# One exponential of 2048 columns for 20 score visits, and a second order of all queues, in a two-layer attention and MLP kernel

## The chip, the cores and the metric

The kernel runs on one core of a Trainium2 chip. The engines are named as in the profile: PE multiplies matrices, ACT evaluates functions, DVE and POOL work on vectors, and SP issues the DMAs. Each engine works through a queue of its own, and semaphores hold an instruction until what it needs is there. The metric is the device time of one execution in microseconds, the median over several runs. Lower is better.

## The reference

Two layers run over a sequence of 2048 tokens with 512 features, with the same weights in both. A layer is sliding-window attention with 32 heads of 16 features, where a token sees itself and the 255 before it, and then an MLP with 1792 hidden features. Each has a layernorm ahead and adds its result to x.

```python
def _A_ref(x, wqkv, wo):
    H = 32; Dh = D // H; W = 256
    qkv = (x @ wqkv).reshape(B, S, 3, H, Dh).transpose(2, 0, 3, 1, 4)
    scores = jnp.einsum("bhqd,bhkd->bhqk", q, k) * (Dh ** -0.5)
    mask = (idx[:, None] - idx[None, :] >= 0) & (idx[:, None] - idx[None, :] < W)
    p = softmax(jnp.where(mask, scores, -1e9))
    return jnp.einsum("bhqk,bhkd->bhqd", p, v)... @ wo
def _B_ref(x, w1, b1, w2, b2):
    return gelu(x @ w1 + b1) @ w2 + b2
for layer in range(2):
    x = x + _A_ref(_layernorm(x), A_wqkv, A_wo)
    x = x + _B_ref(_layernorm(x), B_w1, B_b1, B_w2, B_b2)
```

## The kernel before

The 2048 tokens are 16 tiles of 128, and two layers make 32 tiles, or 16 blocks of 256 tokens (blocks 0 to 7 are layer one). x stays on the core in X for the whole run, as do all weights after their load. The work of a block b is:

- layernorm of its tiles on DVE and POOL (statistics at L628, normalized tile xn at L650), then a transpose to xnTA, by PE for the first four tiles and by a DMA of SP for the others (L655);
- projections to Q and K (512 columns of PSUM, half of the features each) and to V. QT is copied out by DVE or ACT (L617, L619). KT is copied by DVE with a product with `parmask` (L710), which writes it twice, once with the even and once with the odd heads kept. Va is V; Vs is V shifted by half a tile, made by two DMAs a tile (L725);
- scoring "visits" (`visit`, L758): a visit fills 512 columns for each of four row groups of PE, so four banks of PSUM: a pair gA and a pair gB. L777 are its matmuls. Two exponentials follow on ACT, of 128 x 1024 elements each, one a pair (L784), into the ring E, and then masks on DVE or POOL (L805). A block has ten visits, the first block of a layer five;
- two value products a block (`pv`, L829), each over half of the heads, then transposes, a division by the sums (L838 to L852), the output projection, and the sum into X (L878);
- the MLP in ten jobs of two or four tiles: first product with W1, bias on DVE and gelu on ACT (L901, L904), or both in one activation (L909), then the product with W2 and the sum (L921), in the second layer with a store of the tile by SP.

PSUM has eight banks, shared by all of this. ACT must load a table whenever it changes between exponential and gelu.

Nothing is ordered at run time. The kernel first records all its operations as nodes in the order of the source, and tables at the top of the file then decide: `_ORDER` gives the sequence in which nodes enter their engines' queues, `_ALT` the nodes that go to a second engine (a mask to POOL, a copy to ACT), `_BANKS` the PSUM bank of each allocation, `_TURNS` extra dependencies between two nodes. `_PAD` lists matmul groups that get two more waits ahead of them on PE. Both are on a semaphore value that has long been reached, so they only move the instructions behind them within the pages in which PE's program is fetched. `_Plan.run` applies the tables, and `_Sched.op` derives the waits from what each node reads and writes. At most eight DMAs of SP are open at a time, since each waits for the one eight places ahead.

The code around the scores and the evacuation of K is where the change acts:

Of the kernel before, what the change touches and what calls it, by code (L numbers as in the profile page):

```python
# [7 lines left out]
ALU = mybir.AluOpType  # L8
# [11 lines left out]
class _Sched:  # L20
# [347 lines left out]
]  # L368

_PAD = [  # L370
    127, 761, 1289, 1123, 1124, 1116, 1197, 1673, 1403, 1404, 1405, 1406, 1231, 1250, 1251, 1433, 1556,
]

_BANKS = [
# [75 lines left out]
def bass_interleave_layers__sliding_block__dense_activation_gelu__prompt_kernel(  # L450
# [13 lines left out]
    P = 128  # L464
# [34 lines left out]
    with ExitStack() as kctx:  # L499
# [112 lines left out]
        def piece(cuts, fc):  # L612
            return [lo <= fc < hi for lo, hi in cuts].index(True)
# [390 lines left out]
```

## Time and profile before

| | us |
|---|---|
| median of 3 runs | 433.87 (433.02 to 435.62) |
| the profiled execution's own time | 433.44 |
| its span, first to last instruction | 431.7 |
| PE busy | 410.6 |
| ACT busy | 379.6 |
| DVE busy | 336.0 |
| POOL busy | 217.3 |

Busy time is summed over the span. Matmuls are pipelined, so PE counts as busy also where it runs below its peak. The granted clock of PE was 1.0 in the profiled run. The costliest groups on the other engines are the 300 exponentials (282.4 us of ACT) and the masks (128.3 us on POOL, 49.2 us on DVE). The span in 40 slices, in tenths:

```profile
PE   8978999998999989999999999999999999999997
ACT  2898999999999999999998999999977998998523
DMA  7994412201201114010121211011221004102120
```

PE and ACT are both close to full for most of the span. ACT has room at the start and in the last slices, and the DMA engines are in use mostly in the first tenth, while x and the weights are loaded.

### The profile page before, as it was taken

To read this page: it belongs to the slowest core of one execution; us is meant where nothing else is said; L and a number is where in the kernel's file an instruction comes from. 1 tells how busy PE (TensorE), PEld (TensorE's weight loads), DVE (VectorE), ACT (ScalarE), POOL (GpSimd) and SP (SyncE) were. 2 spreads that over 40 slices of the span, in tenths; PEclk is the share of its full clock that TensorE was granted. 3 is DMA by queue.
4 is the path that set the end of the run, shared out by engine and by line. 5 is a ranking of instruction groups with operands and counts; after the bars stand their busy time and mean duration, and the time that the engine had idled before them with its cause. 6 is when DMAs were issued, how large, how long until landed. Compare 5 with 4: busy or idle time off the path is not lost.

```text
span 431.7 us, 16809 instructions
## 1 busy us (share of the span) xinstructions
PE 410.6 (95%) x7500; PEld 228.0 (53%) x7571; DVE 336.0 (78%) x637; ACT 379.6 (88%) x447; POOL 217.3 (50%) x242
## 2 busy tenths in 40 slices
PE   8978999998999989999999999999999999999997
PEld 4655847644544445463554555465545554444763
DVE  5998897889978778857899687779767675857941
ACT  2898999999999999999998999999977998998523
POOL 5576555466444585435764462613537347332420
PEclk9999999999999999999999999999999999999999
DMA  7994412201201114010121211011221004102120
GB/s 229 297 162 107 125 38 44 51 3 41 58 21 33 26 28 74 20 29 2 40 47 26 34 39 41 17 25 29 56 45 27 2 17 78 50 2 72 43 74 24
DMA packets 49059, 23.50 MB, mean 54 GB/s; under 512 B 34268, under 2 KB 48988, under 8 KB 48988
## 3 DMA queue, kind: packets, MB, share of 16 engines
q1 hardware_dynamic: 48988, 22.43, 22.9%
q8 instruction: 59, 0.97, 0.9%
q14 instruction: 12, 0.10, 0.1%
HBM read 8.00 MB, written 2.10 MB: 23 GB/s over the span
## 4 chain that ended last, share of the span: by engine, by line
PE 68%; ACT 19%; DVE 7%; issue 2%; DMA 1%; POOL 1%; SPq 1%; DVEq 0%
PE ps L676 53%; ACT E L784 15%; PE ps L777 7%; PE ps L829 6%; PE ps L569 2%; ACT gT L909 1%; DMA Vs<-Va 1%; DVE OD L838 1%; ACT gT L904 1%; DVE E L805 1%; DVE QT L617 1%; POOL Nb L846 1%; ACT L909 1%; DVE stat L628 1%; DVE KT L710 1%
## 5 line engine op out<-in xcount | busy, mean ns | idle before, releaser
L784 ACT ACTIVATE E<-ps 128x1024 bf16<-128x1024 f32 x300 | 282.4, 1044 | 18.6 <-PE ps L777 17.8
L805 POOL TENSOR_TENSOR E<-E,mask 128x512 bf16<-128x512 bf16 (+2 forms) x116 | 128.3, 1120 | 105.2 <-DVE E L805 50.4
L676 PE MATMUL ps<-W_sb,gT 128*128 128x512 bf16 x413 | 105.6, 380 | 4.6 <-issue 3.7
L676 PE MATMUL ps<-xnTB,W_sb 128*128 128x512 bf16 (+1 forms) x547 | 101.7, 336 | 1.7 <-issue 0.8
L676 PEld LDWEIGHTS ps<-xnTB,W_sb 128*128 128x128 bf16 x560 | 52.4, 98 | 42.9 <-issue 1.6
L676 PE MATMUL ps<-xnTA,Wqkv_sb 128*128 128x256 bf16 x512 | 67.5, 273 | 1.3 <-DVE xnTA L617 0.5
L777 PE MATMUL ps<-QT,KT 32*128 32x128 bf16 (+3 forms) x1920 | 60.1, 231 | 3.1 <-ACT E L784 1.4
L676 PEld LDWEIGHTS ps<-W_sb,gT 128*128 128x128 bf16 x448 | 38.3, 98 | 43.7 <-issue 4.0
L805 DVE TENSOR_TENSOR E<-E,mask 128x512 bf16<-128x512 bf16 (+2 forms) x120 | 49.2, 434 | 15.0 <-POOL E L805 6.6
L676 PEld LDWEIGHTS ps<-xnTA,Wqkv_sb 128*128 128x128 bf16 x512 | 47.4, 98 | 17.9 <-issue 2.5
L777 PEld LDWEIGHTS ps<-QT,KT 32*128 32x128 bf16 x1920 | 28.2, 92 | 50.5 <-ACT E L784 31.9
L838 DVE STREAM_TRANSPOSE OD<-ps 128x1024 f32<-128x1024 f32 x32 | 39.7, 1242 | 12.2 <-PE ps L829 12.0
L909 ACT ACTIVATE gT<-ps,b1T 128x512 bf16<-128x512 f32 (+1 forms) x80 | 43.0, 605 | 5.6 <-PE ps L676 5.2
L917 POOL TENSOR_TENSOR Xb<-X,b2all 128x512 f32<-128x512 bf16 x32 | 36.8, 1153 | 18.8 <-DVE X L921 12.0
L628 DVE BATCH_NORM_STATS2 stat<-X 128x6 f32<-128x512 bf16 x64 | 43.2, 682 | 2.8 <-DMA X<-in_A_x_dram 2.1
L901 DVE TENSOR_SCALAR gT<-ps,b1T 128x512 bf16<-128x512 f32 (+1 forms) x60 | 36.5, 634 | 7.0 <-PE ps L676 6.6
L829 PE MATMUL ps<-E,Va 64*17 64x192 bf16 (+3 forms) x1920 | 39.5, 230 | 2.2 <-ACT E L784 1.0
L710 DVE TENSOR_TENSOR KT<-ps,parmask 128x1024 bf16<-128x1024 f32 x32 | 38.8, 1212 | 3.4 <-PE ps L676 2.9
L829 PE MATMUL ps<-E,Vs 64*17 64x128 bf16 (+3 forms) x1920 | 38.8, 230 | 0.0
L846 POOL TENSOR_TENSOR Nb<-OD,Rc 128x512 bf16<-128x512 f32 x21 | 22.2, 1056 | 32.5 <-DVE Rc L842 16.0
L650 DVE TENSOR_SCALAR xn<-X,statmv,rstd 128x512 bf16<-128x512 bf16 x64 | 24.4, 402 | 13.4 <-POOL rstd L640 8.3
L921 DVE TENSOR_TENSOR X<-Xb,ps 128x512 bf16<-128x512 f32 x32 | 21.5, 677 | 17.0 <-PE ps L676 16.7
(49 smaller groups left out, 358.2 us busy)
## 6 DMA issues: line engine op xcount, KB each, us to landing
Vs<-Va SPq DMA_DIRECT2D x64, 68.0 KB, 2.1
W_sb<-in_B_w_dram SPq DMA_DIRECT2D x4, 512.0 KB, 4.9
out_dram<-X SPq DMA_DIRECT2D x16, 128.0 KB, 1.8
X<-in_A_x_dram SPq DMA_DIRECT2D x3, 512.0 KB, 6.2
Wqkv_sb<-in_A_wqkv_dram SPq DMA_DIRECT2D x4, 256.0 KB, 6.1
W_sb<-in_B_w_dram SPq DMA_DIRECT2D x2, 384.0 KB, 7.9
W_sb<-in_B_w_dram SPq DMA_DIRECT2D x1, 768.0 KB
Wqkv_sb<-in_A_wqkv_dram SPq DMA_DIRECT2D x1, 512.0 KB, 7.0
```

The costliest lines, as they stand in the source:

```text
L628: add("dve", lambda e, B, t=t, k6=k6: e.bn_stats(stat6[:, k6, :], X[:, t, :]), reads=["X%d" % t], writes=["st%d" % k6], key="bs%d" % (k + j))
L676: r = e.matmul(ps[:, B[g][0], cols], lhsT, rhs, start=st, stop=sp)
L710: add("dve", lambda e, B, g=g, i=i: e.tensor_tensor(out=KT[:, kb, 2 * i : 2 * i + 2].rearrange("p c m a q -> p a (c m) q"), in0=ps[:, B[g] ...
L777: x = e.matmul(ps[:, bk[r], o : o + n], KT[rows, kb, c, m].rearrange("p a q -> p (a q)"), QT[rows, c, q : q + n], start=True, stop=True)
L784: add("act", lambda e, B, g_=g_, gi=gi: e.activation(E[:, 2 * gi : 2 * gi + 2, e0 : e0 + 512], ps[:, B[g_][0] : B[g_][0] + 2, :], AF.Exp, ...
L805: fn = lambda e, B: e.tensor_tensor(out=Ew, in0=Ew, in1=Mw, op=ALU.mult)
L829: x = e.matmul(ps[32 * r : 32 * r + VW, B[g][par], c % 2 * 2 * P + lo : c % 2 * 2 * P + hi], V[rows, (2 * b + m // 2) % VR, c * HC + 2 * r ...
L838: add("dve", lambda e, B: e.transpose(OD[:, s].rearrange("p a c q -> p (a c q)"), ps[:, B[g][0] : B[g][0] + 2, :]), reads=["ps:" + g], wri ...
L846: return e.tensor_tensor(out=Nb[:, s, :].rearrange("p (k a d) -> p a k d", a=2, d=Dh), in0=sums[:, :, :, 0:Dh], in1=rc[:, :, :, None].to_b ...
L901: add("dve", lambda e, B, g=g, fc=fc: e.tensor_scalar(out=gT[:, fc, c0 : c0 + M], in0=ps[:, B[g][0], 0:M], scalar1=b1T[:, fc : fc + 1], sc ...
L909: add("act", lambda e, B, g=g, fc=fc: e.activation(gT[:, fc, c0 : c0 + M], ps[:, B[g][0], 0:M], AF.Gelu_apprx_tanh, bias=b1T[:, fc : fc + ...
L917: add("pool", lambda e, B, t=t, xs=xs: e.tensor_tensor(out=Xb[:, xs, :], in0=X[:, t, :], in1=b2all[:], op=ALU.add), reads=["X%d" % t, "b2a ...
```

## The change

There are five parts.

1. Twenty visits, listed in `_WHOLE`, have one exponential of 2048 columns over all four banks in place of two of 1024. Their banks are used in rising order. The pairs may lie apart, so the access steps from one pair to the other.
2. The copy of K may go to ACT, as two activations with `parmask` as scale, one for each parity. One of the 32 does: the first half of block 0.
3. The second MLP product of tile 31, its sum and its store are split into two halves of 256 columns, with a group of 14 matmuls each.
4. All tables are new: order, second engines, turns, pads and banks. Pads go from 17 to 9. Four more copies of V go to ACT (12 instead of 8), six more masks and one more division to POOL.
5. In the new order of SP the larger weight loads stand behind the first shifts of V and transposes.

The number of table loads on ACT stays 18. The visits of `_WHOLE` are counted over the whole program; the first eight (11, 12, 13, 24, 34, 42, 47, 64) belong to blocks 1 to 6.

```diff
+_WHOLE = [
+    11, 12, 13, 24, 34, 42, 47, 64, 71, 72, 88, 89, 90, 91, 97, 119, 126, 127, 135, 144,
+]
 _PAD = [
-    127, 761, 1289, 1123, 1124, 1116, 1197, 1673, 1403, 1404, 1405, 1406, 1231, 1250, 1251, 1433, 1556,
+    228, 230, 232, 188, 189, 472, 646, 668, 734,
 ]
...
+                def kcopy(e, B, g=g, i=i):
+                    for a in range(2):
+                        x = e.activation(
+                            KT[:, kb, 2 * i : 2 * i + 2, :, a, :].rearrange("p c m q -> p (c m) q"),
+                            ps[:, B[g][0], :].rearrange("p (k q) -> p k q", q=HK), AF.Copy, scale=parmask[:, a : a + 1])
+                    return x
...
-                    reads=["ps:" + g, "parmask"], writes=names, free=[g], key="ke%d_%d" % (b, i))
+                    reads=["ps:" + g, "parmask"], writes=names, free=[g], key="ke%d_%d" % (b, i), alt=(("act", kcopy),))
...
+                whole = first[b] + g in _WHOLE
...
-                    bk = tuple(B[gA]) + tuple(B[gB])
+                    bk = tuple(sorted(tuple(B[gA]) + tuple(B[gB]))) if whole else tuple(B[gA]) + tuple(B[gB])
...
-                for gi, g_ in enumerate((gA, gB)):
+                if whole:
+                    def ex(e, B):
+                        lo, hi = sorted((B[gA][0], B[gB][0]))
+                        d = max(1, (hi - lo) // 2)
+                        return e.activation(
+                            E[:, :, e0 : e0 + 512].rearrange("p (z r) q -> p z r q", z=2),
+                            ps[:].rearrange("p (z r) q -> p z r q", r=2)[:, lo // 2 : hi // 2 + 1 : d],
+                            AF.Exp, scale=SCALE)
+
+                    add("act", ex, reads=["ps:" + gA, "ps:" + gB], writes=grains(e0, 512, "ab"), free=[gA, gB],
+                        key="ex%d_%d_0" % (b, g))
+                for gi, g_ in enumerate(() if whole else (gA, gB)):
...
+                parts = 2 if tau == NT - 1 else 1
+                for z in range(parts):
+                    u, lo, hi = tau + z, D // parts * z, D // parts * (z + 1)
...
```

**The start, on DVE.** The rows are line, operation, what is written and read, and its size; lines of the new file are some three higher up to L660. The queue of DVE from its first instruction, before:

```order
L567 MEMSET gT 128x256
L628 BN_STATS stat<-X 128x6
L630 BN_AGGR statmv<-stat 128x2
L551 TENSOR_SCALAR pidx<-pidx 128x2
L628 BN_STATS stat<-X 128x6
L630 BN_AGGR statmv<-stat 128x2
L628 BN_STATS stat<-X 128x6 x2
L650 TENSOR_SCALAR xn<-X,statmv,rstd 128x512 x2
```

and now:

```order
L570 MEMSET gT 128x256
L631 BN_STATS stat<-X 128x6
L633 BN_AGGR statmv<-stat 128x2
L554 TENSOR_SCALAR pidx<-pidx 128x2
L637 TENSOR_SCALAR rstd<-statmv 128x1
L631 BN_STATS stat<-X 128x6
L633 BN_AGGR statmv<-stat 128x2
L653 TENSOR_SCALAR xn<-X,statmv,rstd 128x512
L637 TENSOR_SCALAR rstd<-statmv 128x1
L631 BN_STATS stat<-X 128x6
```

The first normalized tile stands ahead of the third tile's statistics, and the sum with epsilon (L637) has come over from POOL.

**The start, on PE.** The queue of PE from its first matmul: warm-up matmuls on zeros (from gT), transposes (from ident), projections (from Wqkv_sb), scores (from QT, KT). Before:

```order
L569 MATMUL ps<-gT 128x512 x18
L662 MATMUL ps<-ident,xn 128x128 x8
L676 MATMUL ps<-xnTA,Wqkv_sb 128x256 x8
L662 MATMUL ps<-ident,xn 128x128 x8
L676 MATMUL ps<-xnTA,Wqkv_sb 128x256 x18
L777 MATMUL ps<-QT,KT 128x256 x8
```

and now:

```order
L572 MATMUL ps<-gT 128x512 x12
L665 MATMUL ps<-ident,xn 128x128 x4
L572 MATMUL ps<-gT 128x512
L665 MATMUL ps<-ident,xn 128x128 x4
L572 MATMUL ps<-gT 128x512 x3
L679 MATMUL ps<-xnTA,Wqkv_sb 128x256 x16
L665 MATMUL ps<-ident,xn 128x128 x8
L679 MATMUL ps<-xnTA,Wqkv_sb 128x256 x4
L788 MATMUL ps<-QT,KT 128x256 x8
```

Some warm-up matmuls stand behind the first transposes (two more far behind), sixteen projections instead of eight stand ahead of the second transposes, and the first scoring visit comes after 20 projections instead of 26.

**The start, on ACT and SP.** The queue of ACT from its first instruction, before:

```order
L619 ACT_TABLE_LOAD
L619 ACTIVATE xnTA<-ps 128x4x128 x2
L619 ACTIVATE QT<-ps 128x2x256
L784 ACTIVATE E<-ps 128x2x512
L619 ACTIVATE QT<-ps 128x2x256
L784 ACTIVATE E<-ps 128x2x512 x12
```

and now:

```order
L622 ACT_TABLE_LOAD
L622 ACTIVATE xnTA<-ps 128x4x128
L715 ACTIVATE KT<-ps,parmask 128x8x64 x2
L622 ACTIVATE xnTA<-ps 128x4x128
L806 ACTIVATE E<-ps 128x2x512 x2
L622 ACTIVATE QT<-ps 128x2x256 x2
L806 ACTIVATE E<-ps 128x2x512 x18
```

The two halves of the first K copy stand between the two copies of xnTA, and the first two exponentials stand ahead of two query copies, one of which came over from DVE. SP's queue behind the loads of Wqkv, before:

```order
L577 DMA X<-in_A_x_dram 128x4x512
L598 DMA W_sb<-in_B_w_dram 128x4x512
L596 DMA Wo_sb<-in_A_wo_dram 128x4x512
L607 DMA W_sb<-in_B_w_dram 128x3x512
L598 DMA W_sb<-in_B_w_dram 128x4x768
L725 DMA Vs<-Va 64x544
L655 DMA_TRANSPOSE xnTA<-xn 128x4x128 x2
L725 DMA Vs<-Va 64x544 x3
```

and now:

```order
L735 DMA Vs<-Va 64x544 x2
L580 DMA X<-in_A_x_dram 128x4x512
L658 DMA_TRANSPOSE xnTA<-xn 128x4x128 x2
L735 DMA Vs<-Va 64x544 x2
L599 DMA Wo_sb<-in_A_wo_dram 128x4x512
L735 DMA Vs<-Va 64x544 x2
L658 DMA_TRANSPOSE xnTA<-xn 128x4x128 x2
L601 DMA W_sb<-in_B_w_dram 128x4x512 x2
```

Five loads of x and weights stood ahead of the first shift of V; now they stand behind it.

**Blocks 9 and 10, on ACT.** ACT's queue mostly for the second layer, from the table load behind the gelus of the fourth MLP job to the gelus of the fifth; E is written by exponentials, Va is a copy of V, QT one of Q. Before:

```order
L784 ACT_TABLE_LOAD
L784 ACTIVATE E<-ps 128x2x512 x2
L619 ACTIVATE QT<-ps 128x2x256
L784 ACTIVATE E<-ps 128x2x512 x16
L619 ACTIVATE Va<-ps 128x32x16
L784 ACTIVATE E<-ps 128x2x512 x6
L619 ACTIVATE Va<-ps 128x32x16
L784 ACTIVATE E<-ps 128x2x512 x14
L904 ACT_TABLE_LOAD
```

and now:

```order
L806 ACT_TABLE_LOAD
L806 ACTIVATE E<-ps 128x2x512 x18
L622 ACTIVATE Va<-ps 128x32x16
L806 ACTIVATE E<-ps 128x2x512 x4
L622 ACTIVATE Va<-ps 128x32x16
L806 ACTIVATE E<-ps 128x2x512 x2
L622 ACTIVATE Va<-ps 128x32x16
L806 ACTIVATE E<-ps 128x2x512 x6
L798 ACTIVATE E<-ps 128x4x512 x4
L931 ACT_TABLE_LOAD
```

Both hold the exponentials of the same 19 visits. The copy of Q has gone to another engine, a third copy of V has come, and the last four visits have merged exponentials (128x4x512), one behind the other.

More of the change, by code (lines that the diff above doesn't have):

```diff
@@ L918, in mlp @@
                     reads=["X%d" % t, "b2all"], writes=["Xb%d" % xs], key="xb%d" % tau)
[L919 to L926 removed]
+                parts = 2 if tau == NT - 1 else 1
+                for z in range(parts):
+                    u, lo, hi = tau + z, D // parts * z, D // parts * (z + 1)
+                    g = "y%d" % u
+                    pe_group(g, [(gT[:, fc, c0 + i * P : c0 + (i + 1) * P], W2_sb[:, fc, lo:hi], slice(lo, hi),
+                                  fc == 0, fc == FC - 1) for fc in range(FC)], 1,
+                             [gn(fc) + ["W2_%d" % piece(W2_CUTS, fc)] for fc in range(FC)], key=g)
+                    add("dve", lambda e, B, g=g, t=t, xs=xs, lo=lo, hi=hi: e.tensor_tensor(
+                        out=X[:, t, lo:hi], in0=Xb[:, xs, lo:hi], in1=ps[:, B[g][0], lo:hi], op=ALU.add),
+                        reads=["Xb%d" % xs, "ps:" + g], writes=["X%d" % (t + z)], free=[g], key="ya%d" % u)
+                    if tau >= NT - T:
+                        dma(lambda e, B, t=t, lo=lo, hi=hi: e.dma_start(out[0, t * P : (t + 1) * P, lo:hi], X[:, t, lo:hi]),
+                            ["OUT%d" % (t + z)], reads=["X%d" % (t + z)], key="out%d" % (t + z))
         nextjob = 0
```

8 lines of the change are left out of this document (removed), and 408 rows, old and new, of tables (_ALT, _BANKS, _ORDER, _TURNS).

## The prediction

> **What bounds the kernel now.** I read the page's busy shares first, then its chain of work, then the busy times in four stretches that I cut at the first exponential (12.79 us), at the last exponential that the second value product of block 6 needs (165.50) and at the last value product (401.70). In the stretches each engine has its busy time and, in brackets, its instructions.
>
> ```profile
> PE 410.6 (95%) x7500; PEld 228.0 (53%) x7571; DVE 336.0 (78%) x637; ACT 379.6 (88%) x447; POOL 217.3 (50%) x242
> PE 68%; ACT 19%; DVE 7%; issue 2%; DMA 1%; POOL 1%; SPq 1%; DVEq 0%
> 0.00:12.79 12.79, 11.03 (x69) 6.01 (x70) 8.24 (x23) 3.08 (x5) 6.08 (x20) 1.00 0.84 245
> 12.79:165.50 152.71, 143.05 (x2987) 84.51 (x3009) 131.21 (x248) 148.96 (x177) 90.28 (x96) 1.00 0.31 70
> 165.50:401.70 236.20, 229.64 (x4171) 120.17 (x4196) 182.03 (x339) 217.60 (x245) 113.61 (x120) 1.00 0.17 36
> 401.70:431.70 30.00, 26.84 (x294) 17.28 (x296) 14.49 (x30) 9.96 (x23) 7.35 (x7) 1.00 0.14 41
> ```
>
> Two engines take turns. From 12.79 to 165.50 ACT works 148.96 of 152.71 us, 97.5%, and PE 94%: here ACT sets the pace. From 165.50 on PE is at 97% and ACT at 92%: here PE sets it. The rest of PE's order behind the boundary is fixed work, so time saved on ACT before 165.50 moves the end, and time lost by ACT afterwards costs nothing until ACT's results come too late. The waits of ACT in the two middle stretches (microseconds in total, times, longest) say how much there is to take away:
>
> ```profile
> ACT E L784 <- PE ps L777: 4.4, 8, 0.8
> ACT E L784 <- PE ps L777: 13.4, 27, 1.1
> ```
>
> The first row is the early stretch, the second the late one. So in the paced stretch at most 4.4 us of waiting could go; whatever else is gained there must come from less work on ACT or an earlier start. That is why I expect a change of under one per cent.
>
> **The change part by part, against the profiled execution's own 433.44 us** (span 431.70; the rest, 1.74 us, lies around it and is kept). The median of the three runs is 0.43 us above it.
>
> *The start.* The timeline of DVE, ACT, PE and SP at the start:
>
> ```profile
> 2.17 0.47 SPq L582 DMA_DIRECT2D Wqkv_sb<-in_A_wqkv_dram  x1
> 5.08 1.29 DVE L628 BATCH_NORM_STATS2 stat<-X 128x6 f32<-128x512 bf16 x2 [0.31 <-DMA X<-in_A_x_dram]
> 6.28 0.72 DVE L650 TENSOR_SCALAR xn<-X,statmv,rstd 128x512 bf16<-128x512 bf16 x2
> 8.95 1.05 PE L676 MATMUL ps<-xnTA,Wqkv_sb 128*128 128x256 bf16 x8 [0.52 <-DVE xnTA L617]
> 9.83 0.61 PE L662 MATMUL ps<-ident,xn 128*128 128x128 bf16 x8
> 12.34 0.40 PE L777 MATMUL ps<-QT,KT 32*128 32x256 bf16 x8
> 12.79 1.02 ACT L784 ACTIVATE E<-ps 128x1024 bf16<-128x1024 f32 x1 [0.84 <-PE ps L777]
> Wqkv_sb<-in_A_wqkv_dram SPq DMA_DIRECT2D x4, 256.0 KB, 6.1
> ```
>
> Before, the first normalized tiles (6.28) stand behind two statistics of later tiles (5.08, 1.29 us). In the new order tile 0 is normalized ahead of them, and the wait for xnTA at 8.95 can fall to the landing of the K weights: issue at 2.17 plus the median 6.1 us gives 8.3, 0.65 us earlier. Then PE runs sixteen projections (1.05 us for eight, so 2.1), eight transposes (0.5 beside them) and four projections (0.5) before the first scoring visit: 8.3 + 3.1 = 11.4 instead of 12.34. The copy of K that moves from DVE to ACT fits between: two copies from 9.4 on, at the 0.6 us (616 ns in the row of Va further down) that ACT's other copies of 512 columns last, end near 10.6, while ACT would have waited (its 0.84 us before 12.79 is such a wait). So the first exponential starts 1.0 us earlier. One query copy more stands on ACT before the third exponential and takes back 0.5. Net **-0.5 us**; from 0 (weights land at 8.9) to -1.5.
>
> *One exponential for two.* What a merged instruction saves is the fixed part of one. Rows of the chain give steps from start to start, rows by form give durations:
>
> ```profile
> 49.88 1.55 ACT gT L904 x3
> 125.77 1.89 ACT gT L904 x2
> 82.09 14.86 ACT E L784 x16
> L904 ACT ACTIVATE gT<-gT 128x1024 bf16<-128x1024 bf16 x18 | 18.5, 1056 | 0.7 <-DVE gT L901 0.7
> L904 ACT ACTIVATE gT<-gT 128x512 bf16<-128x512 bf16 x12 | 7.3, 633 | 9.3 <-DVE gT L901 9.3
> ```
>
> The activations of L904 step at 0.517 us for 512 columns and 0.945 for 1024: 0.836 ns a column and a fixed 0.09 us. Sixteen exponentials of 1024 columns step at 0.929, fixed 0.07. By durations (633 and 1056 ns) the fixed part would be 0.21 us, but those overlap in a full queue. I take 0.08. Eight of the 20 merged visits lie ahead of the second value product of block 6: 8 x 0.08 = **-0.6 us** (ends: 0, if four banks are read no faster than two and two, and 8 x 0.21 = -1.7). The other twelve lie where PE paces: 0, hidden by PE's 97%. A merged instruction adds one wait: all four banks of a visit come free at its end, the first pair 0.93 us later than before. Queued behind that pair are the next scoring visit and matmul groups on PE; what this costs is in the count of rings below. The visit's masks read both halves, so they start no later.
>
> The Trainium skill, "ScalarE: Activation LUTs", section "Rules for kernel authors", budgets about 0.3 us for every ACTIVATE plus 0.83 ns an element. The row agrees with its slope (0.836) and not with its fixed part in a full queue (0.07); by the page the eight would save 2.4 us, and the sum would be 1.8 us lower.
>
> *Closed rings between ACT and PE.* In the bank table a visit may be given banks that the exponential directly ahead of its own on ACT has just freed. Then ACT must stand still while PE scores. The rows before three such visits:
>
> ```profile
> 82.09 14.86 ACT L784 ACTIVATE E<-ps 128x1024 bf16<-128x1024 f32 x16 [0.66 <-PE ps L777]
> 112.84 3.77 ACT L784 ACTIVATE E<-ps 128x1024 bf16<-128x1024 f32 x4 [0.51 <-PE ps L777]
> 143.34 12.94 ACT L784 ACTIVATE E<-ps 128x1024 bf16<-128x1024 f32 x14 [0.54 <-PE ps L777]
> ```
>
> Counted in order and bank tables, such visits rise from 14 to 21 in all. Ahead of the boundary three cost idle time before (0.66 + 0.51 + 0.54 = 1.71 us); the new order keeps one there that no table load hides. At the mean of 0.57 that is **-1.1 us** (ends: -1.7, and +1.1 if new waits of the same size appear at two other visits). Behind it they rise from about 10 to 19; I charge 0 while PE paces, and price that below.
>
> *PE's share.* At the second value product of block 6 the new order has 288 full matmuls of 512 columns behind it instead of 285; all else of weight is equal.
>
> ```profile
> 274.71 9.23 PE ps L676 x43
> ```
>
> At 9.23 / 43 = 0.215 us, **-0.6 us** remain less (ends: 0, if ACT's lead is spent on them, and -0.6). The split of the last block's tile 31 into two halves leaves its columns the same, and the last group on PE is still tile 30 in one piece:
>
> ```profile
> 428.84 0.69 DVE L921 TENSOR_TENSOR X<-Xb,ps 128x512 bf16<-128x512 f32 x1 [2.26 <-PE ps L676]
> 429.60 0.33 SPq L925 DMA_DIRECT2D out_dram<-X  x1
> ```
>
> So the tail stays: 0, with the halves' extra store among stores that land beside PE's work.
>
> *Masks and copies between engines.* Six more masks go to POOL, four more value copies to ACT, out of DVE.
>
> ```profile
> L805 POOL TENSOR_TENSOR E<-E,mask 128x512 bf16<-128x512 bf16 (+2 forms) x116 | 128.3, 1120 | 105.2 <-DVE E L805 50.4
> L805 DVE TENSOR_TENSOR E<-E,mask 128x512 bf16<-128x512 bf16 (+2 forms) x120 | 49.2, 434 | 15.0 <-POOL E L805 6.6
> L619 ACT ACTIVATE Va<-ps 128x512 bf16<-128x512 f32 x8 | 4.9, 616 | 0.7 <-PE ps L676 0.7
> ```
>
> A mask that ends last costs 1.12 - 0.43 = 0.7 us more on POOL; POOL is half idle, which hides it, and DVE gains room. 0, from -0.7 to +2.1 (three masks that end last).
>
> *Page fetches, pads, late loads.* The big weight loads now come behind the first value shifts, so they run beside PE's instruction pages.
>
> ```profile
> q8 instruction: 59, 0.97, 0.9%
> PEld ps L829 <- issue: 6.8, 17, 0.8
> W_sb<-in_B_w_dram SPq DMA_DIRECT2D x4, 512.0 KB, 4.9
> ```
>
> 59 pages at 0.9% of 16 engines' 431.7 us make 1.05 us each. No wait that the profile puts to issue is over 0.8 us, and I see no sure page stall in it, so I take 0: a gain of 0.8 at best, a loss of 4.9 us if one page is caught once behind a whole load.
>
> The Trainium skill, "Runtime: NRT & Kernel Launch", section "Instruction fetch mechanics", says that the sequencer streams pages ahead and that crossing one is mostly hidden. The trace does not contradict it (0.8 us at most); by it the move of pages is worth nothing, which is my 0.
>
> **Sum:** -0.5 - 0.6 - 1.1 - 0.6 = -2.8, so 433.44 - 2.8 = 430.6; on the footing of the median 431.1. I say **430.7 us**.
>
> **Rivals.**
> - *No change.* PE's own waits follow ACT's. PE is at 94% in the early stretch; if value products wait for POOL masks (three at 0.7 us) and the start's 0.5 stays with the weights, -2.8 becomes about -0.2: 433.2. For it: DVE's masks waited 6.6 us for POOL. Against it: DVE loses work.
> - *Slower: the late rings decide.* These are the rows of ACT near the end:
>
> ```profile
> 392.21 1.94 ACT L784 ACTIVATE E<-ps 128x1024 bf16<-128x1024 f32 x2 [1.14 <-PE ps L777]
> 395.02 5.84 ACT L784 ACTIVATE E<-ps 128x1024 bf16<-128x1024 f32 x6 [0.87 <-PE ps L777]
> 401.81 1.24 PE ps L829 x100
> ```
>
>  Nine more rings behind 165.50 at 0.7 us add 6.3 us of idle ACT, four of them in a row at merged visits of blocks 9 and 10, three in blocks 14 and 15. ACT has 236.2 - 217.6 = 18.6 us of room there, which speaks against it, but the end has little: the last exponential is over at 395.02 + 5.84 = 400.86, and the value product that needs it follows at 401.8 (last row, of the chain), 0.9 us later. It decides once ACT's results come after PE has run out of other matmuls: 430.6 + 6.3 = 436.9.
> - *Faster still.* The fixed part is nearer 0.21 us (another -1.1) and the start brings 1.5: 428.5.
> - *The page part backfires:* one page behind a load, 430.6 + 4.9 = 435.5.
>
> **How the numbers follow.** Forecast 0.44; faster still 0.16; no change 0.26; late rings 0.09; pages 0.05. About 0.5%, 2.2 us, is what a measurement of this kernel tells from no change; that is 431.7 to 436.0. The first two make faster 0.60; no change and 0.02 of the page case make same 0.28; the late rings and the other 0.03 of the page case, which with a second page lies over 436, make slower 0.12. The range runs from 427.5, 1 us under "faster still" for its own spread, to 435.5, the page case. It takes in each unknown cost at either end alone; it leaves out the late rings and all gains at their ends together.
>
> **What would show it.** Right: first exponential near 11.8 us; in the first 165 us fewer than eight waits of ACT for scores; the merged rows stepping at about 1.78 us; the second value product of block 6, which before starts here,
>
> ```profile
> 168.34 0.11 PEld L829 LDWEIGHTS ps<-E,Va 64*17 64x17 bf16 x8 [0.42 <-DVE E L805]
> ```
>
> near 166; PE still at 97% behind it. Wrong: a merged step over 1.86 us; waits of L777 on ACT grown over 20 us in all with value products late behind them; idle PE before a value product with a POOL mask or an issue named; a later first exponential, with weights named before it.

## The result and the profile after

The changed kernel takes 437.93 us, median of six runs (436.86 to 438.67), against 434.92 for the kernel before on the same chip (433.02 to 436.02). The ratio is 1.0072, 95% interval 1.0044 to 1.0101: **slower by 0.7%**, where 0.7% faster was forecast. The time lies outside the range. The profiled execution took 437.75 us, its span is 435.9 against 431.7 before: 4.2 us to be found.

First the sums of the page and its chain of work, for the kernel after:

```profile
PE 413.7 (95%) x7517; PEld 230.0 (53%) x7585; DVE 332.2 (76%) x630; ACT 382.5 (88%) x433; POOL 223.5 (51%) x245
PE 68%; ACT 10%; DVE 9%; DMA 4%; POOL 3%; issue 3%; SPq 2%; DVEq 0%; POOLq 0%
```

Shares of busy time are as before. PE's 413.7 is 3.1 us more, although the matmuls cover the same columns as before (the halves of tile 31 make 14 more of them, at half the width): some lasted longer. "issue" went from 2 to 3% of the chain. Then the four stretches, cut at the same events as before (first exponential, here 0.05 us behind its start; last exponential that the second value product of block 6 needs; last value product). The columns are start and end, length, then busy time and instructions of PE, its weight loads, DVE, ACT and POOL, then granted clock, share of the DMA engines, GB/s:

```profile
0.00:10.79 10.79, 9.55 (x62) 5.14 (x63) 6.99 (x22) 3.68 (x6) 5.28 (x18) 1.00 0.80 239
10.79:164.80 154.01, 144.74 (x2982) 85.26 (x3005) 133.18 (x258) 150.26 (x171) 83.53 (x88) 1.00 0.32 71
164.80:406.18 241.38, 232.88 (x4199) 121.20 (x4223) 177.29 (x321) 218.95 (x238) 126.22 (x133) 0.99 0.18 34
406.18:435.88 29.70, 26.50 (x304) 18.36 (x306) 14.74 (x30) 9.62 (x22) 8.50 (x8) 1.00 0.18 54
```

The start is 2.0 us shorter, the stretch that ACT paces 1.3 longer, the stretch that PE paces **5.2 longer** (241.38 against 236.20), the tail 0.3 shorter. The whole loss lies where the prediction charged nothing, and the granted clock there is 0.99. The chain, cut to block 13, has the largest piece of it (start, length, what ran):

```profile
348.55 0.40 PE ps L788 x12
348.95 0.98 PE ps L679 x8
349.93 1.03 PE ps L851 x79
350.96 1.77 issue
352.73 0.44 PE ps L851 x19
353.18 0.33 PE ps L788 x12
353.51 0.16 issue
353.67 2.81 PE ps L679 x7
```

In the middle of a value product (79 matmuls, then 19) PE stands still for 1.77 us, and the profile names nothing that it waits for. Behind it seven matmuls take 2.81 us; four of them, on 512 columns, take 1.91 us where four at the 0.215 us of the prediction take 0.86. The stretches around it show why:

```profile
350.70:352.75 2.05, 0.28 (x36) 0.10 (x16) 0.50 (x1) 0.73 (x2) 0.67 (x1) 1.00 0.06 15
352.75:357.00 4.25, 4.09 (x73) 1.90 (x75) 3.48 (x5) 1.94 (x2) 0.76 (x2) 0.65 0.13 29
```

The other engines run dry as well, and then the granted clock is 0.65 for 4 us.

What releases PE is in the DMA queues. The page's row for the queue of instruction pages (packets, MB, share) over the whole span:

```profile
q8 instruction: 59, 0.97, 1.0%
```

and the same queue from 350.1 to 351.6 us:

```profile
q8 instruction: 1, 0.02, 5.6%
```

59 pages serve 7517 + 7585 = 15102 matmuls and weight loads, about 256 each. Counted in steps of 256, PE stood at the end of a page. It had entered that page at 346.55. For most pages the packet of the next one starts 0.8 to 1.2 us after such a crossing; here it ran from 350.16 to 351.50, 3.6 us after it, and PE went on at 352.73. By the same count, which is good to about half a microsecond, a request more than 3 us late is no rarity: some seven of the 59 in this profile and some five in that of the kernel before, and but for this one none stops PE for a microsecond. Here PE was through with its page in 4.4 us (346.55 to 350.96), less than the 3.6 and the packet's 1.3 together; a page lasts 435.9 / 59 = 7.4 us on average. So the first theory: **page fetches that come too late**, in block 13 and perhaps elsewhere, and the half clock behind them. The rival: the twenty merged exponentials, or the closed rings that they make.

To place gains and losses I use PE's lag: the time reached at the start of a value product, less the work that PE has done by then, each kind of matmul priced at its shortest steady step, with the same prices for all kernels. It grows by whatever PE loses (first value product of block 0, second of block 6, and so on; worked out from the traces, us; the last four rows are kernels of the experiments below):

```
               block 0   6 (2nd)  7 (2nd)  13 (2nd)  14 (1st)  15 (2nd)
before           5.7      21.2     22.4     29.6      30.6      31.8
after            5.5      20.1     21.8     29.4      33.7      35.8
pads ahead       5.8      21.7     23.5     31.7      32.4      34.3
loads moved      5.1      20.9     22.6     30.2      32.6      34.2
all mended       5.1      19.9     21.8     29.7      30.4      31.8
before, late     5.7      24.3     25.3     32.5      33.4      34.6
```

After had a lead of 1.1 us in block 6, 0.2 in block 13, and lost 3.3 us more than before between two value products.

### The profile page after: what moved, and what is told of

Same layout as the page of the kernel before. It is cut to its first block, busy times and chain, and to the rows that moved or that the text cites. A ratio compares the mean times of both kernels' runs of the same rounds, so it can differ in the third digit from the quotient of the medians.

```text
span 435.9 us, 16834 instructions
## 1 busy us (share of the span) xinstructions
PE 413.7 (95%) x7517; PEld 230.0 (53%) x7585; DVE 332.2 (76%) x630; ACT 382.5 (88%) x433; POOL 223.5 (51%) x245
## 4 chain that ended last, share of the span: by engine, by line
PE 68%; ACT 10%; DVE 9%; DMA 4%; POOL 3%; issue 3%; SPq 2%; DVEq 0%; POOLq 0%
PE ps L679 53%; PE ps L788 8%; ACT E L806 6%; PE ps L851 6%; POOL E L827 2%; DMA xnTA<-xn 2%; DMA Vs<-Va 1%; PE ps L572 1%; DVE KT L720 1%; DMA xnTB<-xn 1%; ACT E L798 1%; DVE E L827 1%; DVE OD L860 1%; ACT gT L931 1%; DVE xn L653 1%
## 5 line engine op out<-in xcount | busy, mean ns | idle before, releaser
L806 ACT ACTIVATE E<-ps 128x1024 bf16<-128x1024 f32 x260 | 245.0, 1034 | 20.8 <-PE ps L788 19.7
L827 POOL TENSOR_TENSOR E<-E,mask 128x512 bf16<-128x512 bf16 (+2 forms) x122 | 134.7, 1119 | 109.0 <-DVE E L827 50.7
L679 PE MATMUL ps<-W_sb,gT 128*128 128x512 bf16 (+1 forms) x429 | 109.4, 376 | 3.8 <-issue 3.3
L679 PE MATMUL ps<-xnTB,W_sb 128*128 128x512 bf16 (+1 forms) x546 | 103.2, 336 | 2.8 <-issue 0.9
L679 PEld LDWEIGHTS ps<-W_sb,gT 128*128 128x128 bf16 x462 | 40.5, 98 | 43.3 <-issue 5.8
L827 DVE TENSOR_TENSOR E<-E,mask 128x512 bf16<-128x512 bf16 (+2 forms) x114 | 47.1, 436 | 17.4 <-POOL E L827 7.8
L939 POOL TENSOR_TENSOR Xb<-X,b2all 128x512 f32<-128x512 bf16 x32 | 36.8, 1154 | 21.5 <-DVE X L948 6.9
L720 DVE TENSOR_TENSOR KT<-ps,parmask 128x1024 bf16<-128x1024 f32 x31 | 37.8, 1218 | 9.5 <-PE ps L679 8.8
L798 ACT ACTIVATE E<-ps 128x2048 bf16<-128x2048 f32 x20 | 37.8, 1889 | 3.1 <-PE ps L788 3.0
L868 POOL TENSOR_TENSOR Nb<-OD,Rc 128x512 bf16<-128x512 f32 x22 | 23.3, 1058 | 30.9 <-DVE Rc L864 17.2
L643 POOL TENSOR_TENSOR rstd<-rstd,mhalf 128x2 f32<-128x2 f32 (+1 forms) x33 | 22.9, 693 | 25.1 <-DVE rstd L637 13.6
```

The costliest lines, as they stand in the source:

```text
L679: r = e.matmul(ps[:, B[g][0], cols], lhsT, rhs, start=st, stop=sp)
L720: add("dve", lambda e, B, g=g, i=i: e.tensor_tensor(out=KT[:, kb, 2 * i : 2 * i + 2].rearrange("p c m a q -> p a (c m) q"), in0=ps[:, B[g] ...
L798: return e.activation(E[:, :, e0 : e0 + 512].rearrange("p (z r) q -> p z r q", z=2), ps[:].rearrange("p (z r) q -> p z r q", r=2)[:, lo // ...
L806: add("act", lambda e, B, g_=g_, gi=gi: e.activation(E[:, 2 * gi : 2 * gi + 2, e0 : e0 + 512], ps[:, B[g_][0] : B[g_][0] + 2, :], AF.Exp, ...
L827: fn = lambda e, B: e.tensor_tensor(out=Ew, in0=Ew, in1=Mw, op=ALU.mult)
L939: add("pool", lambda e, B, t=t, xs=xs: e.tensor_tensor(out=Xb[:, xs, :], in0=X[:, t, :], in1=b2all[:], op=ALU.add), reads=["X%d" % t, "b2a ...
```

## Experiments

**The change once more, and its pages moved.** Three kernels on one chip. The first is the change as it is; the others get 48 more pads, ahead of the place (325 to 344 us) or behind it (353 to 372 us). A pad's waits have long been met; it only moves the boundaries behind it. Excerpts of the edits of `_PAD`, ahead and then behind:

```diff
     228, 230, 232, 188, 189, 472, 646, 668, 734,
+    2275, 2276, 2277, 2279, 2280, 2281, 2282, 2516, 2517, 2518, 2519, 2476, 2477, 2478, 2479, 2382, 2383,
...
```

```diff
     228, 230, 232, 188, 189, 472, 646, 668, 734,
+    2409, 2410, 2411, 2305, 2306, 2307, 2308, 2412, 2309, 2310, 2311, 2312, 2313, 2314, 2315, 2316, 2317,
...
```

> The changed kernel, unchanged. Theory 'page': in its profile PE stood still for 2.03 us in the second value product of block 13 (350.7 to 352.7 us) with an instruction page landing 1.2 us before it went on, and PE was some 3.7 us later behind it than ahead of it. If that belongs to the order, it recurs at the same matmul, with 1.5 to 2.5 us, and the time is 437 to 439. Rival 'chance': the stall was one execution's; then it is missing here, and the time of 437.9 has another cause. The granted clock was 0.996 in that profile and 1.0 in the other runs at the same time, so the half clock behind the stall need not recur.

> The changed kernel with 48 more pads on matmul groups between 325 and 344 us, so that the page boundaries from there on fall 48 instructions earlier in the program. The request for the page that was late is then no longer held behind the wait of the scoring visit 14_2 for ACT. Theory 'page': no stall in the second value product of block 13, the time falls by 2 to 4 us, to 434.2 (434 to 436). Rival 'rings': the loss comes from ACT waiting for scores in blocks 14 and 15; then the time stays at 437.9, or 0.5 more for the pads.

> Control for the pads: the same number, 48, on the groups directly behind the second value product of block 13 (353 to 372 us), so that its own page boundary stays where it is. Theory 'page': the stall stays, 437.9 plus 0 to 0.5. If pads as such make it faster, 434 to 436 would show here too.

| | median us | ratio to before | standstill in block 13 |
|---|---|---|---|
| change again, 12 runs | 437.35 | 1.0068 (1.0044 to 1.0092) | yes |
| pads ahead, 12 runs | 436.22 | 1.0047 (1.0025 to 1.0069) | no |
| pads behind, 6 runs | 439.04 | 1.0097 (1.0061 to 1.0133) | yes |

The chain of the kernel with pads ahead, at the same value product:

```profile
351.21 0.98 PE ps L682 x8
352.19 1.23 PE ps L854 x100
353.43 0.33 PE ps L791 x12
```

The value product runs through in 1.23 us where it took 1.03 + 1.77 + 0.44, and its page was fetched 1.0 to 1.6 us after the crossing, by the count. Over all profiles of the change and its variants the standstill is in 5 of 5 that keep the change's pages there, and in 0 of 5 that move them. So the place of the page boundary decides whether PE stands still here, and pads as such do not. Pads ahead lies just over the 434 to 436 that I expected, pads behind over its 437.9 to 438.4. The times agree in order, but their intervals overlap, so the size comes from the traces: lag between blocks 13 and 14 grows by 0.7 instead of 4.3. The change again, whose profiled execution took 442.19 us, the longest of the twelve, had two more standstills, of 2.0 us at a page at the end of block 1 and of 2.4 us before an MLP job at 172 us, where its weight loads wait 2.12 us for a transpose, as PE does in the kernel with pads behind (2.13 us); pads ahead kept 1.5 us of the first, which lies far ahead of all pads added.

**The merged exponentials undone.** Pads ahead, and each of the twenty exponentials again as two, side by side, each freeing its own pair:

```diff
-_WHOLE = [
-    11, 12, 13, 24, 34, 42, 47, 64, 71, 72, 88, 89, 90, 91, 97, 119, 126, 127, 135, 144,
-]
+_WHOLE = []
```

> The kernel with 48 pads ahead, and every one of the 20 merged exponentials undone: two of 1024 columns, one behind the other at the same place of ACT's queue, in the same banks, each freeing its own pair. My sum gave the merge 0.08 us each and charged only the eight ahead of the second value product of block 6: then 0.6 us more than with pads alone. Rival 'PE paces throughout': 0 to 0.2 us more. Rival 'merging costs, since four banks come free at once': faster by 0.3 to 1 us than with pads alone.

436.03 us (ratio 1.0053, 1.0029 to 1.0078), against 436.22 with them merged. The exponentials on the page, merged and split:

```profile
L809 ACT ACTIVATE E<-ps 128x1024 bf16<-128x1024 f32 x260 | 245.4, 1033 | 19.3 <-PE ps L791 18.1
L801 ACT ACTIVATE E<-ps 128x2048 bf16<-128x2048 f32 x20 | 37.8, 1889 | 3.2 <-PE ps L791 3.2
```

```profile
L818 ACT ACTIVATE E<-ps 128x1024 bf16<-128x1024 f32 x300 | 282.7, 1037 | 21.6 <-PE ps L800 20.4
```

245.4 + 37.8 = 283.2 us of ACT merged, 282.7 split; idle 22.5 and 21.6. The part that names the change is worth nothing here, neither a gain nor the loss.

**A page behind loads, on both sides.** In the change two loads (second half of W2, x of tiles 12 to 15; entries 51 and 54 of `_ORDER`) are issued at 48.5 and 49.1 us, beside the page at the end of block 1. One kernel takes them out of there, to entry 41 of the order (this and the later excerpts of tables show neighbouring entries, not whole lines of the file):

```diff
-    65, 39, 67, 30,
+    65, 39, 51, 54, 67, 30,
...
-    407, 276, 51, 262, 413, 277, 260, 263, 54, 636,
+    407, 276, 262, 413, 277, 260, 263, 636,
```

Another puts them there in the kernel *before*:

```diff
-    220, 373, 54, 211,
+    220, 373, 211,
...
-    253, 341, 51, 287,
+    253, 341, 287,
...
-    392, 364, 281,
+    392, 364, 51, 54, 281,
```

> The changed kernel with the two loads that SP issues at 48.5 and 49.2 us (a piece of W2, and x of tiles 12 to 15, 512 KB each) issued at 7 us instead, behind the last load of Wqkv. In the repeat of the changed kernel and in both padded ones the instruction page requested in the second value product of block 1 came 2.9 to 3.6 us after the boundary instead of 2.0, while these loads were in flight, and PE stood still for 1.4 to 2.0 us at the output projection of tile 2 (54 to 55 us). Theory 'page behind loads': that standstill is gone, the page comes about 1 us after the boundary, and the median falls by 1.0 to 1.8 us against the unchanged kernel's 437.4, to 435.5 to 436.5; the standstill in block 13 stays. Rival 'loads are innocent': the page is as late as before, no change (437 to 438). Rival 'the start pays': the loads delay Wqkv, the first exponential comes 0.5 us or more later and eats it.

> The reverse test: the kernel before, with the same two loads moved from 29.6 and 45 us to behind the second value shifts, at about 48 us, as in the changed kernel. Theory 'page behind loads': the page requested in the second value product of block 1 (fetched at 50.46 us so far) is caught behind them, PE stands still for 1 to 2 us near 53 to 55 us, and the median rises by 0.5 to 1.8 us, to 434.7 to 436. Rival 'loads are innocent': no change, 434.1.

The change with the loads moved: 436.90 us (1.0067, 1.0043 to 1.0091), no measurable gain. Its page is fetched 1.4 us after the crossing, against 1.7 to 3.6 in the six profiles with the loads in place, three of which stand still there for 1.3 to 2.0 us; with the loads moved none is left. Block 13 stays (1.65 us). The kernel before with the loads late is the clean test: 436.13 us, ratio **1.0049 (1.0027 to 1.0071)**. DMA in forty slices from 49.0 to 54.5 us, late and as it was:

```profile
DMA  9960395139999999999999999997700000000000
```

```profile
DMA  9949995000400000000000000000000000000400
```

Here the page came from 52.90 to 54.00, just as the loads ended; as it was, from 50.46 on. PE stands from 53.6 to 55.46:

```profile
53.20 0.12 PEld L785 LDWEIGHTS ps<-QT,KT 32*128 32x128 bf16 x8 [0.21 <-issue]
55.46 0.77 PEld L684 LDWEIGHTS ps<-xnTA,Wqkv_sb 128*128 128x128 bf16 x8 [2.14 <-ACT E L792]
```

The row names an exponential, since one ended 0.2 us before. But in the kernel before, which differs in the place of the two loads alone, the same eight matmuls start ahead of the first exponential and without a wait:

```profile
53.15 1.05 PE L676 MATMUL ps<-xnTA,Wqkv_sb 128*128 128x256 bf16 x8
53.84 3.77 ACT L784 ACTIVATE E<-ps 128x1024 bf16<-128x1024 f32 x4
```

So they do not need it, and such a name has to be read against what the instructions read and write. The lag is 2.8 to 3.1 us larger in every column behind it, and the span 2.9 us longer: lost early, it was not made good.

**All three places mended.** 24 pads ahead, the two loads moved, and one transpose (entry 1126) ten places earlier in the order, because of that wait for a transpose at 172 us. It was run in two series; a last kernel has the other loads, too, back where before has them (49, 45, 42, 53 and 43 early, 51 and 54 near 30 us):

```diff
-    1355, 1280, 1394, 1359,
+    1355, 1280, 1126, 1394, 1359,
...
-    887, 1354, 1126, 1296,
+    887, 1354, 1296,
```

```diff
-    65, 39, 67, 30,
+    65, 39, 49, 45, 42, 53, 43, 67, 30,
...
```

> The changed kernel with all three places mended: 24 pads ahead of the second value product of block 13 (338 to 344 us), the two loads at 7 us, and in SP's order the transpose of tile 10 for the MLP moved ahead of that of tile 19 for the projections (its landing held PE for 1.8 us at 174 us in two of four profiles). Theory 'arrivals': none of the three standstills, excess of PE at the second value product of block 15 near 31.5 to 32.5 us against 31.8 in the kernel before; median 433 to 434.5, so no worse than before and 3 to 4 us under the changed kernel. Rival 'rings': ACT's waits for scores in blocks 14 and 15 hold the end, 436 or more. My recorded sum, if the page part alone was wrong, would ask for 431.

> The mended kernel once more. Its profiled execution took 433.8 us, level with the kernel before, but its median was 435.5 (433.8 to 438.0). Theory 'arrivals': other executions meet a standstill of 1 to 2 us at one of a few places where a page or a transpose has under half a microsecond to spare; then this profile, if slower than 434.5, shows one that the first did not. Rival 'something steady': the profile is slower throughout, with no single step of over 0.8 us in PE's lag.

> The mended kernel with the larger loads of x and weights back where the kernel before has them: five between 7 and 12 us, ahead of the first value shift, and x of tiles 12 to 15 and a piece of W2 near 30 us. In the second profile of the mended kernel PE waited 1.7 us at the first value product of block 1 (36.9 us) for a shift of V that had been issued beside four weight loads. Theory 'arrivals': that wait falls to 0.8 us or less, as in the kernel before, and no early page comes late: the median falls under the mended kernel's 435.2 to 435.5, to 433.3 to 434.5, level with or up to 0.3% under the kernel before. Rival 'loads at the start collide': Wqkv arrives later and the first score moves from 10.2 towards 12; then 435 or more.

435.47 us (1.0048, 1.0027 to 1.0069), 435.17 (1.0016, 0.9995 to 1.0036), and with all loads back 434.80 (**1.0005, 0.9985 to 1.0025**). The first two medians lie over the 433 to 434.5 that I expected, the last over its 433.3 to 434.5, and the forecast's gain did not appear. The second profile of the mended kernel (435.48 us) shows one loss that the first did not, as theory 'arrivals' asked: the weight loads of block 1's first value product wait 1.86 us for a shift of V. The early and late stretch of the first:

```profile
10.70:164.70 154.00, 144.59 (x2989) 85.40 (x3011) 133.05 (x258) 150.19 (x171) 83.54 (x88) 1.00 0.33 71
164.70:402.20 237.50, 231.08 (x4192) 120.81 (x4215) 176.98 (x321) 218.01 (x236) 126.23 (x133) 1.00 0.18 34
```

The late stretch is 3.9 us shorter than the change's, 1.3 longer than before. Its profiled execution took 433.8, and its lag ends at before's 31.8. The last kernel is level with before and its interval lies clear of the change's: pages, loads and that transpose together cost about 0.7%, and what is left of the change gains nothing that can be measured. How much each of the steps from the change to this kernel brings, the overlapping intervals do not say.

**The start.** In the change the first K copy goes back to DVE, the rest unchanged; in the kernel before, the K copy alone goes to ACT; and the kernel before gets the change's first 108 entries of `_ORDER`, with their second engines (K copy included) and banks.

In `_ALT`, of the change and of the kernel before (with kcopy added):

```diff
-    60, 62, 66, 79, 84, 108,
+    60, 62, 66, 79, 108,
...
```

```diff
-    69, 74, 108,
+    69, 74, 84, 108,
...
```

> The changed kernel with the first copy of K back on DVE in place of two activations. By my account the start's gain comes from the order, and the copy on ACT costs nothing since ACT waits there: first exponential unchanged near 10.8 us. Rival 'the copy is the gain': it comes 0.5 us or more later, towards 12.

> One edit of the change alone on the kernel before: the first K copy as two activations on ACT, nothing else moved. In the changed kernel putting it back on DVE made the first score 1.4 us later. Theory 'a lead of PE is kept to the end': first score 0.3 to 0.8 us earlier than 12.34 us and the median 0.2 to 0.8 us under before (ratio 0.998 to 0.9995). Rival 'it needs the order around it': the copy stands behind the two copies of xnTA on ACT and ends no earlier than DVE's, first score at 12.3 or later, no change or up to 0.5 us slower.

> One part of the change alone: the kernel before with the changed kernel's start (the first normalized tile ahead of later statistics, the first K copy on ACT, the new order of the first projections and warm-ups), and everything behind the first 108 nodes as before, PE's pages included. In the profiles the changed kernel is 2.0 us ahead on ACT and 0.6 us ahead on PE by the second value product of block 0, and none of its three standstills can arise here. Theory 'arrivals ate the gains': the start is worth 0.7 to 1.5 us at the end, median 432.4 to 433.2 (ratio 0.997), first exponential near 10.8 us. My recorded term for the start was 0.5. Rival 'the lead is absorbed': PE's fixed work and the waits behind it take all of it back, 433.9, no change.

First exponentials of the change and of the change without the K copy on ACT:

```profile
8.58 1.26 ACT L715 ACTIVATE KT<-ps,parmask 128x512 bf16<-128x512 f32 x2 [1.44 <-PE ps L679]
10.74 1.94 ACT L806 ACTIVATE E<-ps 128x1024 bf16<-128x1024 f32 x2 [0.41 <-PE ps L788]
```

```profile
12.19 1.94 ACT L807 ACTIVATE E<-ps 128x1024 bf16<-128x1024 f32 x2 [0.51 <-PE ps L789]
```

My theory here, that the copy's engine does not matter, was wrong: 1.4 of the 2.0 us of early start come from it. Yet the kernel without it took 436.89 in its one run, no more than the change. In the kernel before, the copy alone gives 435.05 (1.0013, 0.9998 to 1.0028), no gain where 0.998 to 0.9995 was expected: the first exponential comes 0.6 us earlier and the lead is gone by block 1. The change's start before the old order gives 435.91 (1.0035, 1.0019 to 1.0051), where 432.4 to 433.2 was expected. Its first exponential comes at 11.87, not near 10.8, and at the seam PE waits for a copy of Q on DVE (0.52 us) and one of V (0.53). It is 1.4 us behind in block 0, and 1.4 behind in block 15. It tests the seam, not the start, so what the start alone is worth at the end stays open.

**What a merge costs where the ring is tight.** The kernel before with merged exponentials at 37 visits up to visit 64, nothing else moved:

```diff
+_WHOLE = [
+    2, 3, 5, 6, 8, 9, 11, 13, 15, 16, 17, 19, 21, 22, 23, 24, 25, 28, 29, 31, 33, 36, 44, 45, 47, 48, 49, 50, 51,
+    52, 53, 54, 56, 57, 58, 59, 64,
+]
```

> The merge alone, and more of it: the kernel before with one exponential in place of two for 37 visits up to block 6, where ACT sets the pace (every visit there whose pairs are neighbours), in the same places of the queue and the same banks; PE's pages move by 3 instructions at most. By my recorded term, 0.08 us each, ACT would be 3.0 us earlier at the second value product of block 6 and the end 3 us earlier, 431.4. By the steps seen in the changed kernel (1.774 against twice 0.904) it is 37 x 0.034 = 1.3 us on ACT; theory 'arrivals and PE bound it': of that 0 to 1 us reaches the end, 433.4 to 434.4. Rival 'banks come free late': PE waits for banks 0.9 us longer at many of the 37, its waits for ACT ahead of block 6 rise over the 7.3 us of before, and the time is 435.5 or more.

451.91 us: **1.0418 (1.0399 to 1.0437)**, far off. ACT's waits for scores up to 185 us (us in total, times, longest):

```profile
ACT E L808 <- PE ps L790: 11.1, 18, 1.4
ACT E L800 <- PE ps L790: 9.2, 17, 0.6
```

and two visits in a row on its timeline:

```profile
73.95 1.88 ACT L800 ACTIVATE E<-ps 128x2048 bf16<-128x2048 f32 x1 [0.51 <-PE ps L790]
76.36 1.88 ACT L800 ACTIVATE E<-ps 128x2048 bf16<-128x2048 f32 x1 [0.53 <-PE ps L790]
```

20.3 us of waiting against 4.4 before; a visit steps at 2.41 us where two halves step at 1.86. All four banks come free at once, and ACT then stands while PE scores into them. The change's eight early ones sit where this hardly happens (0.3 us of waiting in all), its other twelve where PE paces. PE's own waits for exponentials rise as well, from 3.9 to 18.5 us, as the rival 'banks come free late' asked: the two engines take turns instead of working side by side.

## Why the prediction was wrong, by its steps

**Page fetches, pads, late loads: "so I take 0". This step failed**, and with it the sign. The working looked for stalls in the trace of before ("no wait that the profile puts to issue is over 0.8 us"), but the change moves every boundary, so that trace speaks only of boundaries that no longer exist. The rival at 0.05 had the direction; its mechanism (a page behind a load) is shown by the late loads in the kernel before, 2.1 us by its ratio. The larger loss in the profiled execution of the change, in block 13, came with almost no DMA beside it (share 0.06 in that stretch), so the rival's condition was too narrow. There the standstill of 1.8 us and the 3.4 us of half clock behind it make 3.3 of the 4.0 us of lag by which after ends behind before. The other five executions have a granted clock of 1.0 on record and take 436.86 to 438.67 all the same, so the half clock is that one execution's share and not what the median rests on; how those five split their loss is not on record.

The Trainium skill, "Runtime: NRT & Kernel Launch", section "Instruction fetch mechanics", says that pages of 256 instructions are fetched ahead and that a crossing is mostly hidden. The count agrees (15102 / 59 = 256, with the waits left out), and so does "mostly": at most two of some 59 pages cost over 1 us in any profile here. For those the measured 1.77 us decides.

**The sum of -2.8** would still have failed, since the mended kernel is level. Its terms:

- *The start*, -0.5: the first exponential came at 10.74, earlier than the 11.8 forecast and 2.0 before the old 12.79; the projections, forecast for 8.3, began at 7.60. But the term's other half, copies that come back onto ACT, was too small. ACT's copies of Q between the first exponential and block 6's second value product, before and after:

```profile
L619 ACT ACTIVATE QT<-ps 128x512 bf16<-128x512 f32 x5 | 3.1, 621 | 0.0
```

```profile
L806 ACT ACTIVATE E<-ps 128x1024 bf16<-128x1024 f32 x114 | 107.0, 1043 | 2.6 <-PE ps L788 2.0
L798 ACT ACTIVATE E<-ps 128x2048 bf16<-128x2048 f32 x8 | 15.2, 1898 | 0.3 <-PE ps L788 0.3
...
L622 ACT ACTIVATE QT<-ps 128x512 bf16<-128x512 f32 x7 | 4.2, 611 | 0.3 <-PE ps L679 0.3
...
L622 ACT ACTIVATE Va<-ps 128x512 bf16<-128x512 f32 x3 | 1.8, 611 | 0.8 <-PE ps L679 0.8
```

  Two more, 1.1 us, where the term charged one at 0.5.
- *One exponential for two*, -0.6: a merged one does step as forecast, 1.77 us,

```profile
32.96 1.88 ACT L798 ACTIVATE E<-ps 128x2048 bf16<-128x2048 f32 x1
34.73 1.02 ACT L806 ACTIVATE E<-ps 128x1024 bf16<-128x1024 f32 x1
```

  but the early exponentials take 107.0 + 15.2 = 122.2 us against 121.4 before for the same 130 halves. The saving of 0.1 each is not in the sum; why not, the rows do not say. With the split kernel's 282.7 against 283.2, the term is 0.
- *Closed rings*, -1.1: ACT's early waits for scores fell as forecast, from 4.4 us in eight to 2.3 in eight shorter ones. Waits for V (0.8) and Q (0.3) came in, and ACT's idle time in the stretch is 154.01 - 150.26 = 3.75, before 152.71 - 148.96 = 3.75. One wait gave way to another: 0.
- *PE's share*, -0.6: right in itself; by block 6's second value product after has done 0.7 us more of PE's work (288 full matmuls against 285).
- *So that value product* starts at 167.90 instead of 168.34, not near 166: a lead of 0.4 us in time and, with PE's share, 1.1 in lag. The lead is 0.2 by block 13, without a page's help: the prediction took for granted that behind the boundary PE's order is fixed work, and it is not quite: in the late stretch PE's matmuls wait 0.8 us for transposes in after, and none before.
- *The late rings*: ACT's late waits for scores grew from 13.4 to 17.7 + 2.7 us, past the 20 that I had named as a sign. PE's matmuls waited for ACT 0.5 us in that stretch before and 0.7 after (its weight loads, which run ahead, 19.7 and 21.5), so they cost next to nothing, as charged. The sign was badly chosen.
- *The tail*, 0: right within 0.3 us.

**Open:** what held the page in block 13 for 3.6 us. PE's queue stood at a scoring visit that waits for ACT when it might have been asked for, which fits, but no run tests it. Single executions of one kernel spread over some 4 us and only one of each is profiled, so how often each standstill strikes is not known, nor is the 0.3% between the two series of the mended kernel explained. The last mended kernel's profiled execution took 437.53 us, far over its median, so that its level time is shown by the times alone.

## What to carry to other kernels

A reordering moves every instruction-page boundary of PE, so a trace of the kernel before cannot price it at zero: leave 2 to 3 us (an estimate from the standstill of 1.8 us here and the 2.9 us that the late loads cost) for a page caught badly on a kernel where one engine is full to 97%, look first at pages that PE runs through fast, then move the boundary with pads and see. A gain on the engine that paces is only there if the engine's whole busy and idle time in the stretch falls; count every instruction that changes engine, and expect one removed wait to be replaced by the next. Merge instructions over all buffers of a ring only where the next user of the ring does not stand behind them.

## What the hardware showed that I had not expected

- A page landed 1.2 us (block 13) and 1.5 us (late loads: 54.00 to 55.46) before PE went on; its own transfer took 1.3 and 1.1.
- The half clock behind a standstill is not tied to its length alone. Of the change, second by second from 353 us on:

```profile
353.00:354.00 1.00, 0.84 (x37) 0.53 (x17) 0.73 (x1) 0.44 (x1) 0.00 (x0) 1.00 0.37 86
354.00:355.00 1.00, 1.00 (x5) 0.32 (x3) 1.00 (x2) 1.00 (x2) 0.00 (x0) 0.53 0.00 0
355.00:356.00 1.00, 1.00 (x4) 0.29 (x2) 0.97 (x3) 0.50 (x1) 0.00 (x0) 0.50 0.00 0
356.00:357.00 1.00, 1.00 (x27) 0.51 (x26) 0.79 (x2) 0.00 (x0) 0.76 (x2) 0.50 0.00 0
357.00:358.00 1.00, 1.00 (x8) 0.42 (x5) 0.80 (x3) 0.93 (x2) 0.17 (x1) 0.77 0.00 0
```

  The clock falls only 1.3 us after PE resumed (352.73 to 354.06) and stays at 0.50 for 3.4 us. The loads-moved kernel, with weight loads idle for 1.65 us at the same place (1.95 in the change), kept 1.00. So did the kernel before with late loads, after 2.14 us: its clock is not on record, but its 512-column matmuls behind the standstill step at 0.216 us, the full rate.
- What seems to count is where the standstill falls in time. In the traces' clock records each half clock that ends within a run lasts 3.41 us, and each change lies a whole number of such steps behind the first (102 in the change, 49 and 103 in the change again). Cut at these steps, PE was busy for 1.28 to 1.64 us of the step ahead of a half clock in four cases (change, change again twice, pads behind). It was busy for 1.74 to 1.94 us in the steps with the standstill of block 13 where the clock stayed full (K copy on DVE, pads behind, loads moved). The 2.0 us at the end of block 1 in the change again fell into two steps, busy for 2.40 and 2.48, and cost no clock. One case does not fit: the last mended kernel lost the clock at 31.1 us behind a step with 1.99 us, so PE's busy time in the profile is not the whole measure.

The Trainium skill, "TensorE: Matmul & The Clock Gate", section on the HAM clock gate, gives windows of about 3.4 us of activity or idleness that switch the clock between full and half. The 3.4 us at half agree; that the clock falls after less than 2 us of idleness within such a step does not follow from it.
